# Two store streams move from ScalarE's to SyncE's DMA queue, and the planner of the order gets spare time

## The chip, the cores and the metric

The kernel runs on one core of a Trainium2 chip. The metric is device time in microseconds (us) of one execution; the median of three runs before is 1178.59 us (1177.14 to 1179.32). The profiled execution took 1177.89 us, and its span, from the first to the last instruction of the program, is 1176.0 us. The engines are named as the profile names them: PE (matmul), DVE (VectorE), ACT (ScalarE), POOL (GpSimd) and SP (SyncE, which computes nothing here and only issues DMAs).

## The reference

Two layers, each applied twice in the order A, B, A, B with residual sums, on `x` of 2048 tokens by 640 channels, in float32:

```python
def _A_ref(x, wqkv, wo):            # 32 heads of 20, W, dil = 8, 2
    q, k, v = split(x @ wqkv)
    idx = pos[:, None] - dil * arange(W)[None, :]          # 8 keys, two tokens apart
    logits = einsum("bhsd,bhswd->bhsw", q, k[idx]) * scale  # masked where idx < 0
    o = einsum("bhsw,bhswd->bhsd", softmax(logits), v[idx])
    return o @ wo

def _B_ref(x, w1, b1, w2, b2):      # 640 -> 1536 -> 640
    h = gelu(layernorm(x) @ w1 + b1)
    return h @ w2 + b2

x = A_x
x = x + _A_ref(layernorm(x), A_wqkv, A_wo)
x = x + _B_ref(layernorm(x), B_w1, B_b1, B_w2, B_b2)
...                                 # the same two lines once more
```

## The kernel before

**Tiling.** A layer's tokens are cut into four units: even and odd tokens (the dilation is two) by two halves of 512 tokens each. With two rounds of layers there are eight units, n = 0 to 7, and a unit has four tiles (t = 0 to 3) of 128 tokens. Every float32 operand of a matmul is split into a high and a low float16 part and the product is made of three passes, so that one logical product over 640 channels is 15 matmuls.

**One unit.** The normalized tokens are transposed by DMA into `yT` (from the tile `w`, L570). PE makes the projected values in four groups of heads (`qkvp`, L602, 15 matmuls each; n, t, g). ACT copies each product from PSUM (`ps`, three banks) to `ev` (three buffers, L617), and a store writes two token tiles of a group from `ev` to a DRAM buffer `spill` (`put`, L623; 8 per unit, 64 in all). A fetch reads them back with their halo into `qk` and `v` (L642), DVE computes the attention of a group G = 4n + g (L684 to L722), and the result is split into `ohl` (L732). Its four tiles are transposed by DMA into `yT` (`oT`, L745), PE multiplies by `wo` (`wop`, L756, eight products of 15 matmuls per unit, through the same three banks `ps`), and DVE adds each product to the residual `xf` (L762). A layer norm follows and again a transposition (L570), and then the unit's MLP: per block of 128 hidden channels a first product (`hp`, L810, its weights in `c1`), GELU and the split on ACT and DVE (L816, L819, L821), and a second product into accumulators (`out`, L831, weights in `c2`).

**Weights of the MLP.** In the first 170 us or so the 24 blocks of `w1` and `w2` are loaded (L451), split into two float16 parts by ACT and DVE (L425, L426) into `c1` and `c2`, and stored to the DRAM buffers `mw` (L467, in `prep_m`; 24 stores). From then on the MLP loads its blocks from there into three buffers each (L803, 216 loads).

**What sets the order.** The instructions of all units are not issued where the code makes them: `Plan.run` collects them as operations with an engine, a duration, a priority and what they need, and lays them out on a time axis. It takes the engine and operation that can start first. The operations are then issued in the order of these planned starts. Each engine works its own list strictly in order, and waits at an instruction until what this needs is there. For a DMA the planner assumes a time from its issue to its first packet (`REACH`), a rate that transfers in flight share (`SHARE` when two queues are at work), and a time from the last packet to the landing (`LAND`). An operation that needs a transfer is planned for the landing (`start`, with `LAG["sp"]` = 0.05 us). These figures are the planner's; on the chip only the order remains of them.

**Queues.** DMAs are issued from SP (loads, fetches, transpositions, outputs) and from ACT (the 64 `put` and the 24 `mw` stores), so that a store's wait for its data stands in ACT's list, and every other DMA's wait in SP's.

Of the kernel before, what the change touches and what calls it, by code (L numbers as in the profile page):

```python
# [64 lines left out]
class Plan:  # L65
# [9 lines left out]


    AHEAD = 3.0
    REACH = 0.45
    LAND = 1.4

    SHARE = 1.15

    LETS = ("pv", "hlo", "lo", "at", "xb")

# [24 lines left out]
    def run(self):  # L109
        when = {}  # L110
        waiting = {}
        ready = {}
        left = {}
        for o in self.ops:
            left[o["n"]] = len(set(o["need"]))
            for k in set(o["need"]):
                waiting.setdefault(k, []).append(o)
            if not left[o["n"]]:
                ready.setdefault(o["eng"], []).append(o)
        clock = {e: 0.0 for e in self.LAG}  # L120
        table = None
        port, shut, before = 0.0, [], None
        order = []


        soon, queues, late = [], {}, []
        seen = 0.0

        def done(o, end, lag):
            for u in o["use"]:  # L130
                self.users[u] -= 1
                self.last[u] = max(self.last.get(u, 0.0), end + lag * (u[0] != "pr" or o["eng"] != "dve"))
                if not self.users[u]:
                    self.free[u[0]].append((self.last[u], self.slot[u]))
            for k in o["give"]:
                when[k] = (o["eng"], end, bool(o["move"]))
                for w in waiting.pop(k, ()):
                    left[w["n"]] -= 1
                    if not left[w["n"]]:
                        ready.setdefault(w["eng"], []).append(w)  # L140

        def heads():
            return [q[0] for q in queues.values() if q]

        def turn():
            h = heads()
            return sum(x[1] for x in h) * (self.SHARE if len(h) > 1 else 1.0)

        def event():

            h = heads()
            return min([b for b, _ in soon] + [e for e, _ in late]
                       + ([seen + max(0.0, min(x[0] for x in h)) * turn()] if h else []), default=math.inf)

        def advance(t):
            h = heads()
            if h:
                turns = (t - seen) / turn()
                for x in h:
                    x[0] -= turns  # L160
            for x in h:
                if x[0] < 1e-9:
                    queues[x[2]["eng"]].pop(0)
                    late.append((t + self.LAND, x[2]))
            for b, o in [v for v in soon if v[0] <= t]:
                soon.remove((b, o))
                queues.setdefault(o["eng"], []).append([*o["move"], o])
            for e, o in [v for v in late if v[0] <= t]:
                late.remove((e, o))
                done(o, e, self.LAG["sp"])  # L170
            return t

        def start(o):
            t = clock[o["eng"]]
            if o["lazy"]:
                t = max(t, seen - self.AHEAD + sum(x[0] * x[1] for q in queues.values() for x in q)
                        + sum(v["move"][0] * v["move"][1] for _, v in soon))
            if o["pair"] and o["eng"] == "dve":
                t = max(t, port)
            for k in o["need"]:  # L180
                e, w, moved = when[k]
                w = w + (self.LAG["sp"] if moved else self.LAG[e] if e != o["eng"] else 0.06 * (e != "pe"))
                t = max(t, w)
            if o["pair"] and o["eng"] == "pool":
                for i, (a, b) in enumerate(reversed(shut)):
                    if t >= b:
                        break
                    if a <= t:
                        t = b + 0.1 * (i == 0)
                        break  # L190
            new = {}
            for u in o["use"]:
                if u in self.slot:
                    t = max(t, self.since[u])
                else:
                    fs = self.free[u[0]]
                    if u[0] in self.ORDERED and self.line[u[0]][self.turn.get(u[0], 0)] != u:
                        return None
                    i = new.get(u[0], 0)
                    if i >= len(fs):  # L200
                        return None
                    t = max(t, sorted(fs)[i][0])
                    new[u[0]] = i + 1
            return t

        total = len(self.ops)
        while len(order) < total:
            best = None
            for e, ops in ready.items():
                pick = None  # L210
                for o in ops:
                    t = start(o)
                    if t is None:
                        continue
                    key = (max(t - o["wait"], clock[e] + 0.05), o["prio"], o["n"])
                    if pick is None or key < pick[0]:
                        pick = (key, t, o)
                if pick and (best is None or (pick[1], pick[0]) < (best[1], best[0])):
                    best = pick
            then = event()  # L220
            if best is None and then == math.inf:
                raise RuntimeError(f"the plan is stuck: {[u for u in self.slot if self.users[u]]}")
            if best is None or then <= best[1]:
                seen = advance(then)
                continue
            _, t, o = best
            e = o["eng"]
            ready[e].remove(o)
            d = o["dur"]
            if o["table"] and o["table"] != table:  # L230
                table = o["table"]
                d += self.SWITCH
            for u in o["use"]:
                if u not in self.slot:
                    fs = self.free[u[0]]
                    fs.sort()
                    self.turn[u[0]] = self.turn.get(u[0], 0) + 1
                    self.since[u], self.slot[u] = fs.pop(0)
            o["at"] = t
            order.append(o)  # L240
            clock[e] = t + d
            if o["move"]:
                soon.append((t + self.REACH + 0.2 * (o["dur"] > 1), o))
                continue
            if e == "dve":
                kind = o["give"][0][0]
                if o["pair"]:
                    if shut and t - shut[-1][1] < 0.05 and before != "pv" and kind not in self.LETS:
                        shut[-1][1] = t + d
                    else:  # L250
                        shut.append([t, t + d])
                before = kind
            elif e == "pool" and o["pair"] and d > 1:
                port = t + d
            done(o, t + d, self.LAG[e])
        order.sort(key=lambda o: o["at"])
        self.time = max(clock.values())
        self.order = order
        return order
# [15 lines left out]
def sliding_dilated_then_mlp_kernel(  # L275
# [99 lines left out]
        plan.add(by, 0.1 if by == "act" else 0.38, prio, emit, need, give, use, move=(kb * 1e3 / 16 / packet, packet_time(packet)), lazy=lazy)  # L375

    def dma_transpose(prio, emit, need=(), give=(), use=()):
        plan.add("sp", 1.45, prio, emit, need, give, use, move=(80, packet_time(256) + 0.0045))

    def mm(cols, n, prio, emit, need=(), give=(), use=()):  # L380
        plan.add("pe", cols / 2400.0 + 0.0028 * n, prio, emit, need, give, use)
# [80 lines left out]
    def prep_m(f, i, prio):  # L462
        ck = (f"c{i + 1}", ("prep", f))
        src = (lambda: B_w2[f * P:(f + 1) * P]) if i else (
            lambda: B_w1.rearrange("(k p) c -> p k c", p=P)[:, :, f * P:(f + 1) * P])
        prep_rows(("m", f, i), prio, src, lambda: tile_of(*ck)[:, 0], lambda: tile_of(*ck)[:, 1], [ck])
        dma(328, prio - 5, lambda: nc.scalar.dma_start(mw[i][f], tile_of(*ck)),  # L467
            need=[("lo", ("m", f, i))], give=[("mw", f, i)], use=[ck], by="act")

    def turn(prio, t, name, key, nk, yk):  # L470

# [113 lines left out]
    def qkv(n):  # L585
# [6 lines left out]
        for k, (g, b) in enumerate(halves):  # L592
# [27 lines left out]

            def put(g=g, b=b, ek=ek):
                to = spill[la][par]
                nc.scalar.dma_start(  # L623
                    bass.AP(tensor=to.tensor, offset=to.offset + (g * 3 * ROWS + HALO + start + 2 * b) * GC,
                            ap=[[M * GC, P], [ROWS * GC, 3], [1, 2 * GC]]),
                    tile_of(*ek).rearrange("p a t c -> p a (t c)"))

            dma(P * 6 * GC * 4 / 1e3, -310 + n, put, need=[("ev", n, 2 * b + i, g) for i in range(2)],
                give=[("put", n, g, b)], use=[ek], by="act", packet=8 * GC)

    def fetch(G):
        n, g = divmod(G, NG)
# [319 lines left out]
```

## Time and profile before

| | before |
|---|---|
| median of three runs | 1178.59 us (1177.14 to 1179.32) |
| the profiled execution | 1177.89 us |
| its span | 1176.0 us |
| PE busy | 1157.5 us, 98% |
| DVE busy | 991.6 us, 84% |
| ACT busy | 511.5 us, 43% |
| POOL busy | 150.9 us, 13% |
| granted TensorE clock | 0.998 |

PE is busy in almost every slice of the span, and DVE nearly so until about 990 us, when the last attention is done. Since each engine's list is fixed, the profile is read for the places where PE stands still: what it waited for, and where that was in the lists of DVE and SP. The chain of waits and the list of PE's waits give the places, and the timelines of PE, DVE and SP around each place tell why.

### The profile page before, as it was taken

The page shows a single profiled execution, that of the slowest core. Times are in us where ns is not written, and L with a number is a line of the kernel's source. Part 1 is how long each engine was busy: PE and PEld are TensorE (multiplying, and loading weights), DVE is VectorE, ACT ScalarE, POOL GpSimd, SP SyncE. Part 2 cuts the span into 40 slices and gives each one's busy share as a digit, 9 for nine tenths or more (in the row PEclk, how much of TensorE's full clock was granted, in tenths as well). Part 3 has the DMA queues.
Part 4 walks back from the last instruction along what each step waited for, and adds up shares of the span by engine and source line. Part 5 has one row for each costly group of instructions (what it writes and reads, how often), then busy time and mean ns, then how long its engine had stood idle before and what let it go on. Part 6 is the DMA issues. An engine that isn't in the chain of part 4 may idle for free.

```text
span 1176.0 us, 17291 instructions
## 1 busy us (share of the span) xinstructions
PE 1157.5 (98%) x6902; PEld 626.5 (53%) x6902; DVE 991.6 (84%) x939; ACT 511.5 (43%) x925; POOL 150.9 (13%) x96
## 2 busy tenths in 40 slices
PE   8999999999999999999999999999999999999998
PEld 5444445577554455545554555555456555555554
DVE  7899999999899999999999999999999996311211
ACT  5485334436445345732537352376235423512121
POOL 1020102023011201320221012002120100000000
PEclk9999999999999999999999999999999999999999
DMA  9999997787776477567755865576555845633432
GB/s 294 300 329 283 373 349 195 212 269 243 210 205 196 162 215 188 176 191 190 193 180 177 212 167 188 202 166 186 188 177 161 246 158 128 154 103 102 145 101 79
DMA packets 219773, 235.01 MB, mean 200 GB/s; under 512 B 129884, under 2 KB 170412, under 8 KB 219692
## 3 DMA queue, kind: packets, MB, share of 16 engines
q1 hardware_dynamic: 190636, 194.57, 56.7%
q10 hardware_dynamic: 29056, 39.33, 9.6%
q8 instruction: 54, 0.88, 0.3%
q14 instruction: 27, 0.22, 0.1%
HBM read 158.93 MB, written 44.78 MB: 173 GB/s over the span
## 4 chain that ended last, share of the span: by engine, by line
PE 55%; DVE 28%; DMA 6%; issue 6%; ACT 4%; SPq 1%; POOL 0%; ACTq 0%; DVEq 0%; POOLq 0%
PE ps L602 20%; PE acc L831 14%; PE ps L810 14%; PE ps L756 7%; DVE pr L684 6%; DVE pr L710 6%; DVE pr L718 4%; DVE sm L688 4%; DMA yT<-w 2%; DVE act L821 1%; DMA qk<-spill 1%; ACT junk L528 1%; DMA act<-in_B_w_dram 1%; DVE w L722 1%; ACT junk L524 1%
## 5 line engine op out<-in xcount | busy, mean ns | idle before, releaser
L602 PE MATMUL ps<-wq,yT 128*128 128x480 f16 x1920 | 393.0, 367 | 4.8 <-DMA yT<-w 3.6
L831 PE MATMUL acc<-c,act 128*128 128x512 f16 (+1 forms) x2310 | 331.3, 299 | 1.1 <-DVE act L821 0.6
L810 PE MATMUL ps<-yT,c 128*128 128x512 f16 (+1 forms) x1620 | 328.6, 355 | 0.8 <-DMA c<-mw 0.8
L602 PEld LDWEIGHTS <-yT 128*128 128x128 f16 x1920 | 187.7, 98 | 207.0 <-DMA yT<-w 5.1
L831 PEld LDWEIGHTS <-act 128*128 128x128 f16 x2310 | 181.7, 98 | 143.3 <-DVE act L821 1.2
L810 PEld LDWEIGHTS <-c 128*128 128x128 f16 x1620 | 154.5, 98 | 147.1 <-DMA c<-mw 1.2
L816 ACT ACTIVATE act<-ps,b 128x512 f32<-128x512 f32 (+1 forms) x108 | 68.7, 637 | 272.4 <-PE ps L810 268.0
L684 DVE TENSOR_TENSOR pr<-qk 128x2560 f32<-128x2560 f32 x64 | 181.5, 2836 | 4.1 <-DMA qk<-spill 4.1
L710 DVE TENSOR_TENSOR pr<-sm,v 128x2560 f32<-128x2560 f32 x64 | 179.7, 2819 | 0.2
L688 DVE TENSOR_REDUCE sm<-pr 128x128 f32<-128x2560 f32 x64 | 179.5, 2805 | 0.1
L821 DVE TENSOR_TENSOR act<-act 128x512 f16<-128x512 f32 (+1 forms) x108 | 72.3, 671 | 124.1 <-ACT act L819 123.8
L718 DVE TENSOR_TENSOR pr<-pr 128x1280 f32<-128x1280 f32 (+1 forms) x128 | 144.8, 1151 | 0.2
L756 PE MATMUL ps<-wo,yT 128*128 128x320 f16 x960 | 132.4, 299 | 5.9 <-DMA yT<-ohl 3.3
L617 ACT ACTIVATE ev<-ps 128x480 f32<-128x480 f32 x128 | 71.6, 563 | 148.8 <-PE ps L602 137.3
L756 PEld LDWEIGHTS <-yT 128*128 128x128 f16 x960 | 93.7, 98 | 44.4 <-DMA yT<-ohl 4.3
L732 POOL TENSOR_TENSOR ohl<-w,ohl 128x640 f16<-128x640 f32 x24 | 67.1, 2796 | 379.2 <-ACT ohl L729 379.2
L541 POOL TENSOR_TENSOR ln<-ln,half 128x2 f32<-128x2 f32 (+1 forms) x30 | 36.2, 1207 | 451.0 <-ACT ln L538 451.0
L524 ACT ACTIVATE junk<-xf 128x640 f16<-128x640 f32 x56 | 41.1, 734 | 79.2 <-DVE xf L762 60.3
L819 ACT ACTIVATE act<-act 128x512 f16<-128x512 f32 (+1 forms) x108 | 62.4, 580 | 2.6
L568 DVE TENSOR_TENSOR w<-w,w 128x640 f16<-128x640 f32 x60 | 51.2, 874 | 1.5 <-ACT w L566 1.5
L560 ACT ACTIVATE w<-xf,ln 128x640 f32<-128x640 f32 x56 | 49.7, 908 | 1.9 <-DVE w L568 1.6
L566 ACT ACTIVATE w<-w 128x640 f16<-128x640 f32 x60 | 42.7, 727 | 12.5 <-DVE w L568 7.2
(53 smaller groups left out, 515.1 us busy)
## 6 DMA issues: line engine op xcount, KB each, us to landing
c<-mw SPq DMA_DIRECT2D x216, 320.0 KB, 3.2
spill<-ev ACTq DMA_DIRECT2D x64, 480.0 KB, 4.3
qk<-spill SPq DMA_DIRECT2D x32, 880.0 KB, 5.5
v<-spill SPq DMA_DIRECT2D x32, 880.0 KB, 4.5
qk<-spill SPq DMA_DIRECT2D x32, 320.0 KB, 3.2
act<-in_B_w_dram SPq DMA_DIRECT2D x24, 320.0 KB, 5.9
mw<-c ACTq DMA_DIRECT2D x24, 320.0 KB, 5.8
xf<-in_A_x_dram SPq DMA_DIRECT2D x16, 320.0 KB, 6.3
```

The lines of the kernel that those rows point to most:

```text
L602: nc.tensor.matmul(ps, transposed(yk)[:, a * KD + k, t * P:(t + 1) * P], wq[:, b, k, g], start=first and j == 0, stop=last and j == len(to ...
L617: act(3 * GC, -400 + n, lambda i=i, pk=pk, ek=ek: nc.scalar.activation(tile_of(*ek)[:, :, i], tile_of(*pk)[:, :3 * GC].rearrange("p (a c) ...
L684: nc.vector.tensor_mul(tile_of(*pk), w[:, HALO + m + t0:HALO + m + t0 + EH, None, :].to_broadcast([P, EH, W, GC]), windows(w, t0, [GC, W], ...
L688: dve(E, G - 0.7, lambda pk=pk, t0=t0: nc.vector.tensor_reduce(lg(t0, t0 + EH).rearrange("p t w h -> p (t w h)"), tile_of(*pk).rearrange(" ...
L710: nc.vector.tensor_mul(tile_of(*vk).rearrange("p t w (h d) -> p t (w h) d", d=DH), lg(t0, t0 + EH).rearrange("p t w h -> p t (w h)")[:, :, ...
L718: dve(EH * w * GC, G - 0.9, lambda vk=vk, w=w: nc.vector.tensor_add(tile_of(*vk)[:, :, 0:w], tile_of(*vk)[:, :, 0:w], tile_of(*vk)[:, :, w ...
L732: eng.tensor_sub(tile_of(*hk)[:, :, 1, g * GC:(g + 1) * GC], ot(), hi())
L756: nc.tensor.matmul(tile_of(*pk)[:, :D // 2], transposed(yk)[:, a * KD + k, t * P:(t + 1) * P], wo[:, b, k, c * D // 2:(c + 1) * D // 2], s ...
L810: nc.tensor.matmul(tile_of(*pk)[:, :nt], tile_of(*ck)[:, a, k * P:(k + 1) * P], transposed(yk)[:, c * KD + k, t0 * P:t1 * P], start=i == 0 ...
L816: act(nt, -430, lambda pk=pk, h32=h32, e=e: nc.scalar.activation(tile_of(*h32)[:, :nt], tile_of(*pk)[:, :nt], AF.Gelu_apprx_tanh, bias=b1[ ...
L821: dve(nt, -1000, lambda h32=h32, hk=hk: nc.vector.tensor_sub(tile_of(*hk)[:, 1, :nt], tile_of(*h32)[:, :nt], tile_of(*hk)[:, 0, :nt]), nee ...
L831: nc.tensor.matmul(accs[k][:, c0:c0 + n], tile_of(*hk)[:, a, (i - t0) * P:(i - t0 + 1) * P], tile_of(*wk)[:, c, w0:w0 + n], start=first, s ...
```

## The change

Four things are edited.

1. The planner's figures for DMAs: a transfer starts `REACH` = 0.75 us after its issue (or its issue's own duration, if longer) plus a ramp of 0.2 us, lands 0.9 us after its last packet (0.5 us for a transposition) plus 0.7 us before what it used is free, and two queues share at 1.08 in place of 1.15. A transposition's issue is planned at 1.75 us in place of 1.45.
2. Spare time: an operation that needs a transfer is planned 2.0 us after the landing on PE, and 0.7 us after it on ACT, DVE and POOL.
3. The 64 stores of projected values (`put`) are issued from SP.
4. The 24 stores of split weights (`mw`) are issued from SP.

What each instruction computes is unchanged; the lists' order and the queue of 88 stores change. The number of instructions is the same on each engine but for the 88 that go from ACT to SP.

```diff
     AHEAD = 3.0
-    REACH = 0.45
-    LAND = 1.4
-
-    SHARE = 1.15
+    REACH = 0.75
+    LAND = 0.9
+    RAMP = 0.2
+
+    SPARE = {"pe": 2.0, "act": 0.7, "dve": 0.7, "pool": 0.7, "sp": 0.0}
+
+    SHARE = 1.08
...
-                    late.append((t + self.LAND, x[2]))
+                    late.append((t + self.LAND - 0.4 * (x[2]["dur"] > 1), x[2]))
...
-                queues.setdefault(o["eng"], []).append([*o["move"], o])
+                queues.setdefault(o["eng"], []).append([o["move"][0] + self.RAMP / o["move"][1], o["move"][1], o])
...
-                done(o, e, self.LAG["sp"])
+                done(o, e, 0.7)
...
-                w = w + (self.LAG["sp"] if moved else self.LAG[e] if e != o["eng"] else 0.06 * (e != "pe"))
+                w = w + (self.LAG["sp"] + self.SPARE[o["eng"]] if moved else self.LAG[e] if e != o["eng"] else 0.06 * (e != "pe"))
...
-                soon.append((t + self.REACH + 0.2 * (o["dur"] > 1), o))
+                soon.append((t + max(self.REACH, o["dur"]), o))
...
     def dma_transpose(prio, emit, need=(), give=(), use=()):
-        plan.add("sp", 1.45, prio, emit, need, give, use, move=(80, packet_time(256) + 0.0045))
+        plan.add("sp", 1.75, prio, emit, need, give, use, move=(80, packet_time(256) + 0.0045))
...
-        dma(328, prio - 5, lambda: nc.scalar.dma_start(mw[i][f], tile_of(*ck)),
-            need=[("lo", ("m", f, i))], give=[("mw", f, i)], use=[ck], by="act")
+        dma(328, prio - 5, lambda: nc.sync.dma_start(mw[i][f], tile_of(*ck)),
+            need=[("lo", ("m", f, i))], give=[("mw", f, i)], use=[ck])
...
             def put(g=g, b=b, ek=ek):
                 to = spill[la][par]
-                nc.scalar.dma_start(
+                nc.sync.dma_start(
...
             dma(P * 6 * GC * 4 / 1e3, -310 + n, put, need=[("ev", n, 2 * b + i, g) for i in range(2)],
-                give=[("put", n, g, b)], use=[ek], by="act", packet=8 * GC)
+                give=[("put", n, g, b)], use=[ek], packet=8 * GC)
```

The lines of the changed kernel stand three further down than before (L745 becomes L748). What moved is shown at three places.

**SP, ahead of the projection of unit 5** (`oT` of unit 5 is the L745 row; `c` tiles are MLP weights, `qk` and `v` the fetches of groups 26 and 25, `yT2` the tokens of unit 7). Before:

```order
L803 DMA c12_80<-mw05_116 128x1280
L803 DMA c20_81<-mw13_126 128x1280
L803 DMA c10_78<-mw06_117 128x1280
L642 DMA qk0_67<-spill11_138 128x640
L642 DMA qk0_67<-spill11_138 128x1760
L803 DMA c21_82<-mw14_127 128x1280
L745 DMA_TRANSPOSE yT0_72<-ohl0_75 128x10x128 x4
L570 DMA_TRANSPOSE yT2_74<-w3_87 128x10x128
```

With the change:

```order
L806 DMA c12_80<-mw05_116 128x1280
L806 DMA c20_81<-mw13_126 128x1280
L748 DMA_TRANSPOSE yT0_72<-ohl0_75 128x10x128 x4
L645 DMA qk0_67<-spill11_138 128x640
L645 DMA qk0_67<-spill11_138 128x1760
L573 DMA_TRANSPOSE yT2_74<-w1_85 128x10x128
L806 DMA c21_82<-mw14_127 128x1280
L573 DMA_TRANSPOSE yT2_74<-w0_84 128x10x128
```

The four transpositions now stand ahead of two weight loads and of the two parts of a fetch, behind which they stood.

**DVE, ahead of unit 4's projected values** (the L568 rows are the last step before the transposition of its first two token tiles; L821 belongs to the MLP, L710 to L722 to the attention of group 7). Before:

```order
L710 TENSOR_TENSOR pr1_77<-sm1_90,v0_68 128x2560
L821 TENSOR_TENSOR act_66<-act_66 128x256
L718 TENSOR_TENSOR pr1_77<-pr1_77 128x2x640
L821 TENSOR_TENSOR act_66<-act_66 128x256
L718 TENSOR_TENSOR pr1_77<-pr1_77 128x2x320
L722 TENSOR_TENSOR w0_84<-pr1_77 128x320
L710 TENSOR_TENSOR pr0_76<-sm1_90,v0_68 128x2560
L821 TENSOR_TENSOR act_66<-act_66 128x256
L568 TENSOR_TENSOR w2_86<-w4_88,w2_86 128x640
L568 TENSOR_TENSOR w1_85<-w3_87,w1_85 128x640
```

With the change:

```order
L713 TENSOR_TENSOR pr0_76<-sm1_90,v0_68 128x2560
L571 TENSOR_TENSOR w2_86<-w0_84,w2_86 128x640
L824 TENSOR_TENSOR act_66<-act_66 128x256
L571 TENSOR_TENSOR w4_88<-w1_85,w4_88 128x640
L721 TENSOR_TENSOR pr0_76<-pr0_76 128x2x640
L824 TENSOR_TENSOR act_66<-act_66 128x256
L721 TENSOR_TENSOR pr0_76<-pr0_76 128x2x320
```

Both steps moved ahead of six instructions of the attention and the MLP. On PE, the products of unit 4 moved ahead of two pairs of MLP blocks (the second products of blocks 5 and 6 and the first products 20 and 21, 256 tokens wide) at the same place.

**SP, ahead of the MLP part of unit 1** (`yT0` rows are that unit's four transpositions for it; `c` are the weights of the running MLP part, `spill<-ev` the stores of projected values of unit 4). Before, the stores were in ACT's list:

```order
L642 DMA v0_68<-spill01_136 128x1760
L570 DMA_TRANSPOSE yT0_72<-w0_84 128x10x128
L570 DMA_TRANSPOSE yT0_72<-w1_85 128x10x128
L642 DMA qk0_67<-spill01_136 128x640
L642 DMA qk0_67<-spill01_136 128x1760
L570 DMA_TRANSPOSE yT0_72<-w4_88 128x10x128
L570 DMA_TRANSPOSE yT0_72<-w0_84 128x10x128
L803 DMA c21_82<-mw110_133 128x1280
L803 DMA c11_79<-mw01_112 128x1280
```

With the change:

```order
L645 DMA v0_68<-spill01_136 128x1760
L573 DMA_TRANSPOSE yT0_72<-w1_85 128x10x128
L573 DMA_TRANSPOSE yT0_72<-w3_87 128x10x128
L626 DMA spill10_137<-ev2_71 128x3x320
L806 DMA c22_83<-mw18_131 128x1280
L806 DMA c12_80<-mw011_122 128x1280
L806 DMA c20_81<-mw19_132 128x1280
L806 DMA c10_78<-mw00_111 128x1280
L573 DMA_TRANSPOSE yT0_72<-w1_85 128x10x128
L806 DMA c21_82<-mw110_133 128x1280
L573 DMA_TRANSPOSE yT0_72<-w3_87 128x10x128
L806 DMA c11_79<-mw01_112 128x1280
```

A store, four weight loads and no fetch now stand between the second and the third of these transpositions, and the weights of the running part are issued between transpositions that wait for DVE.

## Prediction, made before the changed kernel was run

> **What bounds the kernel now.** I read the busy shares first, then the list of PE's waits, then the timelines around each wait.
>
> ```profile
> span 1176.0 us, 17291 instructions
> PE 1157.5 (98%) x6902; PEld 626.5 (53%) x6902; DVE 991.6 (84%) x939; ACT 511.5 (43%) x925; POOL 150.9 (13%) x96
> 800.00:900.00 100.00, 99.16 (x560) 52.08 (x559) 98.75 (x84) 41.44 (x69) 19.10 (x9) 1.00 0.60 185
> ```
>
> The last row is one stretch of the span, with PE, PEld, DVE, ACT and POOL busy in that order. PE is the bound, and DVE runs beside it at nearly 99% as long as there is attention left. The matmuls are the same before and after the change, so the time moves by what PE stands still, 1176.0 - 1157.5 = 18.5 us, and by the clock it runs at. PE's waits by what ended them (us in total, times, longest):
>
> ```profile
> PE ps L602 <- DMA yT<-w: 3.6, 3, 2.0
> PE ps L756 <- DMA yT<-ohl: 3.3, 2, 2.5
> PE ps L756 <- DVE xf L762: 2.6, 3, 0.9
> PE ps L810 <- DMA c<-mw: 0.8, 1, 0.8
> ```
>
> 7.7 us are waits for a DMA to land, in six places; 2.6 us are waits for DVE to empty a bank `ps`, in three; the rest is the head, small gaps, and 3 us behind the last matmul. The six, on PE, each with its wait at the row's end:
>
> ```profile
> 233.62 1.81 PE L810 MATMUL ps<-yT,c 128*128 128x256 f16 x15 [0.85 <-DMA c<-mw]
> 296.68 7.94 PE L602 MATMUL ps<-wq,yT 128*128 128x480 f16 x30 [1.97 <-DMA yT<-w]
> 424.39 3.84 PE L756 MATMUL ps<-wo,yT 128*128 128x320 f16 x27 [0.83 <-DMA yT<-ohl]
> 502.59 2.60 PE L602 MATMUL ps<-wq,yT 128*128 128x480 f16 x12 [1.25 <-DMA yT<-w]
> 645.98 1.19 PE L602 MATMUL ps<-wq,yT 128*128 128x480 f16 x5 [0.35 <-DMA yT<-w]
> 787.44 12.81 PE L756 MATMUL ps<-wo,yT 128*128 128x320 f16 x93 [2.47 <-DMA yT<-ohl]
> ```
>
> The second of them costs more than its wait. The stretch behind it (PEclk is the number behind POOL's):
>
> ```profile
> 297.30:300.70 3.40, 3.40 (x10) 1.32 (x9) 3.40 (x3) 0.00 (x0) 0.00 (x0) 0.51 1.16 344
> ```
>
> For 3.4 us the granted clock was 0.51: half of 3.4 is 1.7 us lost. It is the only such stretch between the head and the tail.
>
> **The change, part by part.** *The projection of unit 5 (2.47 us).* DVE and SP ahead of it:
>
> ```profile
> 763.22 0.83 DVE L732 TENSOR_TENSOR ohl<-w,ohl 128x640 f16<-128x640 f32 x1 [0.27 <-ACT ohl L729]
> 759.01 16.55 SPq L803 DMA_DIRECT2D c<-mw  x6
> 778.03 0.80 SPq L642 DMA_DIRECT2D qk<-spill  x2
> 779.41 9.84 SPq L745 DMA_TRANSPOSE yT<-ohl  x4
> ```
>
> The data were ready at 764.1, and the first transposition was issued at 779.4, behind weight loads that wait for PE to free a buffer, one in some 3.25 us, and a fetch that waits for DVE. It landed 8.0 us later, at 787.4. In the new list the four stand behind the fifth of the six loads (759.01 + 4 x 3.25 = 772.0) and ahead of the sixth and the fetch. Issue at 772.3 and the median landing of its kind
>
> ```profile
> yT<-w SPq DMA_TRANSPOSE x60, 4.4
> yT<-ohl SPq DMA_TRANSPOSE x32, 3.8
> c<-mw SPq DMA_DIRECT2D x216, 320.0 KB, 3.2
> ```
>
> give 776 to 777. PE comes at 787.4 - 2.5 = 785.0, less one second product of the MLP that now stands behind (3.26 us, a row below): 781.7. The whole 2.47 goes.
>
> *Unit 4's projected values (1.97 us and the slow stretch).*
>
> ```profile
> 282.13 0.42 DVE L821 TENSOR_TENSOR act<-act 128x256 f16<-128x256 f32 x1
> 289.90 1.55 DVE L568 TENSOR_TENSOR w<-w,w 128x640 f16<-128x640 f32 x2
> 852.52 3.24 PE ps L810 x15
> 855.75 3.26 PE acc L831 x24
> ```
>
> DVE's first step moves to where the 282.13 row stands, 289.90 - 282.13 = 7.8 us earlier. PE arrives two pairs of half-width blocks earlier; a full-width pair is 3.24 + 3.26, so two halves are 6.5. The lead grows by 1.3: 0.7 of the wait stays. The slow stretch came behind a wait of 1.97, and none came behind 1.25 or less; behind 0.7 I expect none, and take the 1.7 as gone (bounds: nothing, and 1.7). The Trainium skill, "TensorE: Matmul & The Clock Gate", section "Part 1: The HAM clock gate (the "warmup" mystery)", has the clock halved only after at least one idle window of about 3.4 us. The 0.51 row stands behind an idle time of 1.97, so rule and row differ on the threshold, while the row's length of 3.4 us is the window's. By the rule alone no wait here would have cost clock, the term were nothing and the sum 1174.3.
>
> *The MLP's weights at 233 us (0.85).* The load was issued late, behind a fetch of `v` for which SP waited on DVE. In the new DVE list the step that frees `v` stands ahead of two instructions of 2.8 us, so SP is past it in time: I take 0.85 as gone. *Units 2 and 6 (0.83, 0.35).* The new lists give 0.7 and 1.2 us more lead: 0.6 and 0.35 go. *Unit 5's projected values (1.25).* DVE's step stands 4.2 us later in DVE's list and the products 2.2 later in PE's, 2.0 worse; against it DVE is 2 to 3 us earlier by then, since this idle time of DVE is filled with two instructions of the next group:
>
> ```profile
> 306.69 0.49 DVE L762 SCALAR_TENSOR_TENSOR xf<-ps,xf 128x320 f32<-128x320 f32 x1 [3.12 <-PE ps L756]
> ```
>
> I leave the 1.25 as it is. Gone: 2.47 + 1.3 + 1.7 + 0.85 + 0.6 + 0.35 = 7.3 us.
>
> *The start of unit 1's MLP part (new).*
>
> ```profile
> 333.55 1.55 DVE L568 TENSOR_TENSOR w<-w,w 128x640 f16<-128x640 f32 x2
> 334.62 6.22 SPq L570 DMA_TRANSPOSE yT<-w  x2
> 347.14 3.40 PE L810 MATMUL ps<-yT,c 128*128 128x512 f16 x15
> ```
>
> DVE is ready at 335.1 and PE comes at 347.1, a lead of 12.0. In the new list 9.5 us more of DVE's work stand ahead (three instructions of 2.8 and some short ones), of which the filled 3.1 are won back; PE comes 1.6 later by its list and about 2.2 earlier by the waits gone before: 12.0 - 9.5 + 3.1 + 1.6 - 2.2 = 5.0. One transposition ahead on SP (about 1.6 us, between a fourth of the 9.84 above and less) and 4.4 to land are 6.0: PE waits about 1.0 more, between nothing and 2 (at the 3.1 of issue that two took here). The running part's weights, now issued between these transpositions, wait with them and are in the same 1.0.
>
> *The head.* ACT now splits the third piece of the first weights after it copies the first tokens, not before:
>
> ```profile
> 8.15 0.72 PE L481 MATMUL acc<-ident,w 128*128 128x128 f32 x5
> 8.61 0.87 ACT L425 ACTIVATE wq<-pr 128x800 f16<-128x800 f32 x1 [0.28 <-DMA pr<-in_A_wqkv_dram]
> 9.39 0.74 ACT L487 ACTIVATE yT<-acc 128x512 f16<-128x512 f32 x2
> 10.02 3.34 PE L602 MATMUL ps<-wq,yT 128*128 128x480 f16 x15 [1.15 <-ACT yT L487]
> 11.22 0.88 DVE L514 BATCH_NORM_STATS2 bn<-xf 128x6 f32<-128x320 f32 x2
> ```
>
> The copy can begin at 8.9; the split then ends at 8.9 + 0.74 + 0.87 = 10.5, and the first products start near 10.6, not 10.0. What paces the next tokens is DVE, whose split of the same piece (1.0 us) then ends at 11.5, not 11.2. I take +0.3, between nothing and 0.6.
>
> *The queues.*
>
> ```profile
> L623 ACTq DMA_DIRECT2D spill<-ev x64: 366/367/1044, 20.1 to 853.2; - x64
> ```
>
> 64 issues of 0.37 us, and 24 of the weights at about as much, 33 us in all, leave an engine that is busy 43% of the time and that PE seldom waits for: worth nothing. On SP, which waits more than it issues, the issue time is hidden in its waits. What may cost is that a store waits there for its copy, and everything behind it too; the copy comes about a microsecond behind its product, and most stores stand behind instructions that wait longer. I count nothing; rival B holds the other end. The 2.6 us of bank waits I leave; rival A holds theirs.
>
> **Sum.** -7.3 + 1.0 + 0.3 = -6.0 against the profiled execution's own 1177.89: 1171.9. The median of the runs stands 0.7 above that execution, so 1172.6, said as 1172.5.
>
> Does DVE allow it? At the last projection:
>
> ```profile
> 987.68 0.82 DVE L732 TENSOR_TENSOR ohl<-w,ohl 128x640 f16<-128x640 f32 x1 [0.80 <-ACT ohl L729]
> 988.57 5.99 SPq L745 DMA_TRANSPOSE yT<-ohl  x4
> 992.29 16.46 PE L756 MATMUL ps<-wo,yT 128*128 128x320 f16 x120
> ```
>
> From DVE's end at 988.5 to PE's start are 3.8 us, just a landing: PE can't come earlier here unless its list holds more work ahead, or DVE ends earlier. The new list sets a first product and a quarter of a second one ahead, 3.24 + 0.8 = 4.1 us. The other 1.9 must come from DVE, out of the 3.1 that are filled.
>
> **The rivals.**
>
> *A: the banks take it back (no change).* With three banks and products of 16.46 / 8 = 2.06 us, a residual add of DVE that is late by more than two products holds PE. The new DVE list sets instructions of 2.8 us between the adds of units 1 and 3, where short ones or none stood, and by the lists' shifts an add is then 0.3 to 1.8 us too late at five of the eight projections, some 4.5 us in all: 1172.6 + 4.5 = 1177.1. For it: the planner now believes that PE starts these products 2 us after the landing, and plans DVE's adds accordingly late. Against it: each of these shrinks by what DVE is ahead.
>
> *B: everything waits in SP's list (slower).* Place: the eleven entries of PE that a transposition feeds (the projections of units 1 to 7, the first products of 4 to 7). Price: a store that waits 1.2 us for its copy, with the transposition behind it, costs 1.2 there; with nine hit, and one slow stretch of 1.7, 1172.6 + 10.8 + 1.7 = 1185. It decides from 6.0 / 11 = 0.55 us per entry on. For it: the 15 us for which the transposition at 779 us stood behind others show that SP's list holds up ready work. Against it: only the stores next to a transposition count. The Trainium skill, "DMA: Bandwidth & Descriptors", section "Anatomy of one DMA — SWDGE (gpsimd) path", says that the DMA engines don't wait on semaphores and that every such wait is made by the issuing sequencer. The 779.41 row agrees, and by that rule each store takes its wait along into SP's list.
>
> *C: more goes.* If DVE's earlier time carries through, the other DMA and bank waits go as well: 7.7 + 2.6 - 5.6 = 4.7, and the 1.0 at unit 1: 1172.6 - 5.7 = 1167.
>
> That the change does nothing the chip can see has no chance of its own: the lists differ at the places named.
>
> **Chances.** Forecast 0.49 (its own range 1169 to 1177), A 0.21, B 0.16, C 0.14. A measurement of this kernel tells about 0.2%, 2.4 us, from no change, so 1176.2 to 1181.0 counts as the same. Faster: C, 0.44 of the forecast and 0.04 of A, 0.62. Same: 0.15 of A, 0.04 of the forecast, 0.01 of B, 0.20. Slower: B's rest, 0.02 of A and 0.01 of the forecast, 0.18. The range goes from C's end to what leaves out the larger half of B: 1167 to 1182.
>
> **What would show it.** Right: in PE's waits `yT<-ohl` falls from 3.3 to under 1, `yT<-w` from 3.6 to 1 to 3, with no wait of 2 us at unit 5's projection and no stretch at half clock near 300 us; the new wait is at the start of unit 1's MLP part. A shows as `xf L762` at 6 or more; B as waits on `yT` of 10 or more, with transpositions queued on SP behind L626 rows. I am wrong altogether if PE's waits fall as said and the span doesn't.

## The result, and the profile after

The median of four runs each went from 1178.95 to 1166.35 us, a ratio of 0.9893 (95% interval 0.9867 to 0.992): 12.6 us less, where 6 were forecast. The profiled execution took 1165.98 us, 11.9 less than the one before, and 0.4 less than its median.

The busy times and PE's list of waits after the change (engine, line, what it waited for; us in total, times, longest):

```profile
span 1164.2 us, 17345 instructions
PE 1154.4 (99%) x6902; PEld 625.6 (54%) x6902; DVE 992.3 (85%) x939; ACT 510.2 (44%) x923; POOL 166.8 (14%) x96
PE ps L605 <- ACT wq L428: 2.5, 1, 2.5
PE acc L888 <- POOL ident L400: 1.4, 1, 1.4
PE acc L834 <- DVE act L824: 1.3, 2, 0.8
PE ps L605 <- DMA yT<-w: 0.5, 1, 0.5
PE acc L834 <- DVE xf L869: 0.5, 1, 0.5
PE ps L759 <- DVE xf L765: 0.3, 1, 0.3
```

All line numbers are three higher than before. PE's idle time fell from 18.5 to 9.8 us and its busy time by 3.1, of which 1.7 is the half-clock stretch near 300 us, which is gone; the rest comes from several small differences. `yT<-ohl` went from 3.3 to nothing, `yT<-w` from 3.6 to 0.5, `c<-mw` from 0.8 to nothing, and the banks (`xf`, L762 before, L765 now) from 2.6 to 0.3. The first two rows are the head. Its waits are 3.9 us before (1.4, 1.3 and 1.2 in three rows) and 3.9 now, but in the profiled execution a stretch at half clock has come there that the one before did not have (stretch, length, busy time of PE, PEld, DVE, ACT and POOL with their counts, then the granted clock):

```profile
10.93:14.34 3.41, 3.41 (x10) 1.23 (x9) 3.04 (x10) 0.00 (x0) 1.24 (x2) 0.50 1.15 365
```

The first 15 products start 0.15 us earlier than before (9.87 against 10.02) and take 4.88 us instead of 3.34. PE has made up for it by 15.2 us, since it no longer waits for DVE in between (1.3 us before).

The places that the prediction spoke of, in the timeline after the change (start, duration, engine; a bracket at the end of a row is the engine's wait before it):

```profile
231.21 0.72 PE L834 MATMUL acc<-c,act 128*128 128x512 f16 x4 [0.79 <-DVE act L824]
286.34 15.35 PE L605 MATMUL ps<-wq,yT 128*128 128x480 f16 x75
334.93 0.83 DVE L571 TENSOR_TENSOR w<-w,w 128x640 f16<-128x640 f32 x1
343.47 4.70 PE L813 MATMUL ps<-yT,c 128*128 128x512 f16 x21
496.56 3.62 PE L605 MATMUL ps<-wq,yT 128*128 128x480 f16 x17 [0.53 <-DMA yT<-w]
764.26 6.40 SPq L748 DMA_TRANSPOSE yT<-ohl  x4
773.39 16.46 PE L759 MATMUL ps<-wo,yT 128*128 128x320 f16 x120
975.02 0.83 DVE L735 TENSOR_TENSOR ohl<-w,ohl 128x640 f16<-128x640 f32 x1 [0.80 <-ACT ohl L732]
984.54 5.73 PE L759 MATMUL ps<-wo,yT 128*128 128x320 f16 x41
```

Four rows of PE carry no bracket: unit 4's projected values (286.34) and unit 5's projection (773.39), which had 1.97 and 2.47 before, the start of unit 1's MLP part (343.47), where a new wait was forecast, and the last projection (984.54). A bracket of 0.53 stands at unit 5's projected values (1.25 before), and one of 0.79 (0.28 before) at the start of unit 0's MLP, on an activation that DVE splits late.

The last two rows matter most. DVE's last split ended at 988.5 before and ends at 975.85 now, 12.7 us earlier. PE began that projection at 992.29 and begins it at 984.54, 7.75 earlier, with more of its list ahead of it. The lead of DVE over PE there, from the end of its last split to PE's start, grew from 3.8 to 8.7 us.

Where DVE won its time is seen from its busy time in stretches up to its last split, before and after (stretch, us, DVE busy):

```profile
0.00:100.00 100.00, 86.26 (x111) 1.00 1.00 297
300.00:400.00 100.00, 94.28 (x87) 1.00 0.65 196
700.00:800.00 100.00, 96.50 (x85) 1.00 0.68 191
0.00:988.60 988.60, 953.17 (x880) 1.00 0.72 216
```

After the change, with PE, PEld, DVE, ACT and POOL in that order:

```profile
0.00:100.00 100.00, 96.16 (x519) 49.62 (x520) 90.60 (x113) 64.17 (x125) 15.03 (x21) 0.98 0.98 296
300.00:400.00 100.00, 99.96 (x611) 56.02 (x610) 99.46 (x91) 46.37 (x88) 24.73 (x10) 1.00 0.67 195
700.00:800.00 100.00, 100.00 (x607) 53.91 (x606) 99.45 (x93) 54.44 (x99) 19.80 (x11) 1.00 0.61 182
0.00:975.90 975.90, 969.93 (x5759) 527.36 (x5760) 953.83 (x880) 463.36 (x843) 165.46 (x94) 1.00 0.73 218
```

DVE's work is the same (953.2 and 953.8 us); its idle time ahead of the last split fell from 35.4 to 22.1, by 13.3. Of this, 4.3 lie in the first 100 us, 5.2 between 300 and 400, and 3.0 between 700 and 800. By what ended it, DVE's waits for PE's products of the projections fell by 4.5 up to the last split (7.3 to 2.8 us), those for fetches by 2.4 (4.1 to 1.7), and those for ACT's part of the split of `wo`, in the first 40 us, by 3.5; the rest is spread thin:

```profile
DVE wo L426 <- ACT wo L425: 3.9, 2, 2.8
```

```profile
DVE wo L429 <- ACT wo L428: 0.4, 1, 0.4
```

So about a third of the idle time that went had been a wait for PE.

### The profile page after: what moved, and what is told of

The parts are those of the page before. It is cut to its first block, busy times and chain, and to the rows that moved or that the text cites. A ratio compares the mean times of both kernels' runs of the same rounds, so it can differ in the third digit from the quotient of the medians.

```text
span 1164.2 us, 17345 instructions
## 1 busy us (share of the span) xinstructions
PE 1154.4 (99%) x6902; PEld 625.6 (54%) x6902; DVE 992.3 (85%) x939; ACT 510.2 (44%) x923; POOL 166.8 (14%) x96
## 4 chain that ended last, share of the span: by engine, by line
PE 89%; DVE 7%; issue 2%; DMA 1%; ACT 0%; SPq 0%; DVEq 0%; ACTq 0%
PE ps L605 33%; PE acc L834 23%; PE ps L813 23%; PE ps L759 11%; DVE pr L687 2%; DVE pr L713 1%; DVE pr L721 1%; DVE sm L691 1%; DVE act L824 1%; DMA pr<-in_A_wqkv_dram 1%; DVE xf L869 0%; DMA yT<-w 0%; DVE w L571 0%; DVE w L725 0%; DVE sm L704 0%
## 5 line engine op out<-in xcount | busy, mean ns | idle before, releaser
L735 POOL TENSOR_TENSOR ohl<-w,ohl 128x640 f16<-128x640 f32 x24 | 81.4, 3391 | 410.2 <-ACT ohl L732 410.2
L544 POOL TENSOR_TENSOR ln<-ln,half 128x2 f32<-128x2 f32 (+1 forms) x30 | 39.2, 1306 | 400.1 <-ACT ln L541 400.1
```

What stands on the lines that cost most here:

```text
L735: eng.tensor_sub(tile_of(*hk)[:, :, 1, g * GC:(g + 1) * GC], ot(), hi())
```

## The experiments

Three questions: which part of the change makes the gain; whether DVE or PE holds the end; and what the half-clock stretch hangs on. Ratios are against the kernel before, with 95% intervals.

**The queue alone.** Order of before; only the issuing engine of the two stores is changed, while the planner still takes them for ScalarE's:

```
-        dma(328, prio - 5, lambda: nc.scalar.dma_start(mw[i][f], tile_of(*ck)),
+        dma(328, prio - 5, lambda: nc.sync.dma_start(mw[i][f], tile_of(*ck)),
...
-                nc.scalar.dma_start(
+                nc.sync.dma_start(
```

> The order of before, word for word on every engine, but the 88 stores are issued by SyncE instead of ScalarE, at the same place of the common order. Theory 'order' (the new order with spare time makes the gain): 1176 to 1181, PE's waits on yT stay at 6.9 us and DVE's idle time up to its last split at 35. Rival 'queue' (the stores' way through SyncE makes it, by stores that leave sooner and a ScalarE that issues nothing): 1166 to 1172, waits on yT under 3. Rival B of the prediction (stores hold up what stands behind them on SP): 1182 or more.

0.9999 (0.9988 to 1.001). The stores' way is worth nothing, to within 0.1%.

**The order alone.** The reverse: the order of the change, and the two stores issued by `nc.scalar`.

> The order of the change, word for word on every engine, but the 88 stores are issued by ScalarE as before. Theory 'order': 1164 to 1169, PE's waits on yT under 1.5 us. Rival 'queue': 1172 or more, since ScalarE's 33 us of issues come back and the stores wait behind its activations.

0.9894 (0.9876 to 0.9912): the whole gain. In the landing times of the two kernels (KB each, median us to landing) the queue does show, first the order alone, then the change:

```profile
spill<-ev ACTq DMA_DIRECT2D x64, 480.0 KB, 4.5
```

```profile
spill<-ev SPq DMA_DIRECT2D x64, 480.0 KB, 3.4
```

In the order of the change a store lands 1.1 us sooner through SP's queue (in the order of before 0.4 us: 4.3 and 3.9), and the time is the same. The gain is the order of the instructions; the two stores matter only in that the planner counts them in another engine's list.

**No spare time.** The change with

```
-    SPARE = {"pe": 2.0, "act": 0.7, "dve": 0.7, "pool": 0.7, "sp": 0.0}
+    SPARE = {"pe": 0.0, "act": 0.0, "dve": 0.0, "pool": 0.0, "sp": 0.0}
```

> The change with all spare time at 0; the stores' queue and the new numbers for transfers stay. Theory 'order' in its narrow form (the spare time makes the gain): most of it goes, 1173 to 1181, PE's waits on yT 4 us or more. Rival 'constants' (the plan's new landing times do it, or the queue): 1164 to 1169.

0.9966 (0.9953 to 0.9979): a third of the gain. PE's waits of this kernel:

```profile
PE ps L759 <- DMA yT<-ohl: 4.0, 3, 2.0
PE ps L605 <- DMA yT<-w: 3.9, 2, 3.2
```

**Spare time on one side.** PE's 2.0 alone, and the other engines' 0.7 alone:

> The change, but spare time on TensorE alone (2.0 us; 0 elsewhere). Theory 'spare time on PE cures PE's waits for transpositions': PE's waits on yT under 1.5 us, against 7.9 with no spare time at all and 0.5 with all of it. The time is 1165 to 1172, with some more of DVE's waits for qk<-spill. Rival 'it is the engines' smaller spare time': yT 4 us or more, 1172 to 1178.

> The change, but spare time on ScalarE, VectorE and GpSimd alone (0.7 us; 0 on TensorE). Theory 'spare time on PE': PE's waits on yT 4 us or more, 1171 to 1180. Rival: under 1.5 us, 1165 to 1170.

0.9941 (0.9919 to 0.9963) and 0.9949 (0.9931 to 0.9968). The first is a miss: with PE's spare time alone PE's waits on `yT` stay at 6.8 us, 4.35 of them in front of unit 2's projection. DVE's last split for it ends at 420.5, 12 us later than in the change:

```profile
PE ps L759 <- DMA yT<-ohl: 6.8, 3, 4.4
```

```profile
419.66 0.82 DVE L735 TENSOR_TENSOR ohl<-w,ohl 128x640 f16<-128x640 f32 x1
427.19 1.25 PE L759 MATMUL ps<-wo,yT 128*128 128x320 f16 x4 [4.35 <-DMA yT<-ohl]
```

PE itself came there only 4.7 us later than in the change, wait left out, so that the 2 us by which the planner sets PE later did not cover it.

With the other engines' spare time alone the waits on `yT` are 5.1 us (2.9 on `yT<-ohl`, 2.2 on `yT<-w`), as expected. So neither side alone cures them.

**The planner's other edits.** The stores planned and issued on ScalarE (`by="act"`), with the new spare time and the new numbers; and a profile of the same kernel, for its waits:

> The change with its spare time and its numbers for transfers, but the stores planned and issued on ScalarE as before; so the plan is made anew, and its order differs from both. Theory 'order': 1164 to 1170, as any plan with this spare time. Rival 'queue': 1172 to 1179.

> The kernel planned with the spare time and with the stores on ScalarE, whose time equals that of before, for a look at its waits. If DMA waits are what spare time cures: PE's waits on yT under 2 us, and its loss stands elsewhere (banks, DVE, the clock), some 10 us. If spare time does not cure them: yT 5 us or more.

0.9997 (0.9983 to 1.0011): the gain is gone altogether. That is a miss: 1179.1 us, where any plan with this spare time was expected at 1164 to 1170. It doesn't speak for the rival either, since the queue alone is worth nothing. The profile has no wait on `yT` at all, as expected; the loss is elsewhere:

```profile
PE acc L834 <- DVE act L824: 6.7, 4, 2.8
PE ps L813 <- DMA c<-mw: 1.7, 3, 1.0
PE acc L834 <- DMA c<-mw: 1.4, 1, 1.4
```

These 9.8 us, and two half-clock stretches of 3.4 us behind the waits at 228 and 348 us (2 x 1.7 us), make up for what the transpositions no longer cost. Next, the change with the transfers' numbers of before (the issue and landing times of the diff above are set back as well):

```
-    REACH = 0.75
-    LAND = 0.9
-    RAMP = 0.2
+    REACH = 0.45
+    LAND = 1.4
+    RAMP = 0.0
...
-    SHARE = 1.08
+    SHARE = 1.15
```

> The change with its spare time and its stores on SyncE, but with the numbers for transfers of before (0.45 us to reach the queue, 1.4 to land, 1.15 for shared queues, a transposition's issue 1.45). Theory: PE's waits on yT under 1.5 us, as with any plan that has PE's spare time; whether the time is that of the change hangs on the rest of the order, which no theory foretells: 1164 to 1178. Rival 'the new numbers do it': yT 4 us or more, 1172 or above.

0.996 (0.9943 to 0.9976), with 2.4 us of waits on `yT` (expected under 1.5) and one wait of 4.0 on DVE at unit 0's MLP. And more spare time (3.0 on PE, 1.2 on DVE):

> The change with more spare time (3.0 us on TensorE, 1.2 on VectorE). If what is left of PE's waits is for late data: 1163 to 1166, yT and c<-mw at 0. If spare time is enough already and a larger one only sets DVE's work later for the banks and the units' MLP parts: 1166 to 1175, waits on DVE above 2 us.

0.9908 (0.9893 to 0.9923), 0.4 us on `yT`, no better than the change, with 4.9 us of waits on DVE: the second expectation. Together:

| planned with | PE waits on `yT`, us | ratio |
|---|---|---|
| the order of before | 6.9 | 1 |
| no spare time | 7.9 | 0.9966 |
| PE's alone | 6.8 | 0.9941 |
| the others' alone | 5.1 | 0.9949 |
| both, transfers of before | 2.4 | 0.996 |
| both, stores in ScalarE's list | 0 | 0.9997 |
| both, larger | 0.4 | 0.9908 |
| both: the change | 0.5 | 0.9893 |

The waits are those of one profiled execution of each plan, which lies up to 3.4 us from the median of its runs (with the stores in ScalarE's list, 0.9 us); they say where a plan waits, not what it takes. In these plans it takes spare time on both sides to cure the waits for transpositions. That alone doesn't give the time, since each new plan also waits elsewhere: by its list of waits, 6.7 us on DVE at the MLP with the stores in ScalarE's list, 4.0 there and 2.5 at the banks with the transfers of before. The queue alone gives nothing, and each edit to the plan that was taken away lost about half of the gain or more. Why the plan without the stores in SP's list is worse at the MLP parts was not followed up.

**One wait alone, and two.** In the order of before, only the four transpositions of unit 5's projection are moved ahead of the loads and the fetch they stood behind (rows of SP, shortened):

```
+ L745 DMA_TRANSPOSE yT<-ohl x4
  L803 DMA c<-mw  (three of them)
  L642 DMA qk<-spill x2
  L803 DMA c<-mw
- L745 DMA_TRANSPOSE yT<-ohl x4
```

> The order of before but for four rows on SP: the transpositions of unit 5's projection stand ahead of the three weight loads and the fetch they were queued behind. Theory 'DVE follows' (DVE waits for PE where PE waits for DMA, so that a wait taken from PE moves DVE as well and the gain reaches the end): 2.5 less than before, the span as well; DVE's last split 2.3 earlier; no new wait behind. Rival 'DVE is fixed' (the prediction's step: DVE's last split stays where it is, and PE waits later for what it does not wait for here): 0 to 0.8 less than before, with some 2 us of new waits on yT<-ohl or on the banks behind 790 us.

0.9963 (0.9952 to 0.9974), 4.4 us less, where 2.5 were expected. The profile shows 2.65 of them. Up to the place PE runs 1.6 us later than before (longer waits for a bank at 195 us and for the MLP's weights at 234 us), and behind it 1.1 earlier, with no wait at unit 5's projection:

```profile
767.48 6.17 SPq L745 DMA_TRANSPOSE yT<-ohl  x4
786.37 8.86 PE L756 MATMUL ps<-wo,yT 128*128 128x320 f16 x64
```

DVE does the same: 1.6 us later up to the place, 1.1 earlier behind it. The step comes at its residual add, which before had waited for the product that waited for the transpositions, and now waits no more (before, then here):

```profile
789.69 0.49 DVE L762 SCALAR_TENSOR_TENSOR xf<-ps,xf 128x320 f32<-128x320 f32 x1 [2.27 <-PE ps L756]
```

```profile
788.88 0.49 DVE L762 SCALAR_TENSOR_TENSOR xf<-ps,xf 128x320 f32<-128x320 f32 x1
```

From there on PE and DVE both keep their 1.1 to the end: DVE's last split ended at 987.4 instead of 988.5. The interval, 3.1 to 5.7 us, does not reach down to 2.65; the rest was not followed up.

Next, unit 4's projected values alone: DVE's two splits ahead of one product of 2.8 us, their transpositions ahead of a fetch and two loads.

> The order of before but for unit 4's projected values: DVE's two splits for them stand ahead of one product of 2.8 us and one short step, and their transpositions ahead of the fetch of v and two weight loads on SP. Both theories: the wait of 1.97 us goes. Theory 'the half-clock stretch hangs on this wait': it goes too, 3.7 less than before in all, no stretch at half clock near 300 us. Rival 'the stretch comes anyway' (set by how PE was busy before, not by the wait): 2.0 less. Rival 'DVE is fixed': 0 to 1 less, new waits on yT behind 300 us.

0.9984 (0.9971 to 0.9997), 1.9 us less: the size that the rival 'the stretch comes anyway' gave, though not at its place. The wait of 1.97 and the stretch at half clock near 300 us are gone; 1.11 comes back at the next projection. What is left of it moves DVE as well: across the place PE gains 2.7 us on the order of before and DVE 2.6. And a stretch at half clock has come at another place, behind the wait of unit 5's projection, where before had none:

```profile
781.38:784.79 3.41, 1.32 (x10) 0.99 (x11) 1.78 (x3) 0.74 (x1) 0.00 (x0) 1.00 1.38 164
784.79:788.20 3.41, 3.41 (x15) 1.90 (x14) 1.76 (x2) 0.00 (x0) 0.00 (x0) 0.50 1.11 210
```

Both corrections together:

> Both corrections of the two kernels before, in the order of before. If waits taken from PE add up and reach the end: 6.1 us less than before. If DVE holds the end: 0 to 2 less. What this leaves of the change's 12 us is owed to the rest of the order (the banks, the smaller waits, DVE's idle time).

0.9959 (0.9944 to 0.9973), 4.8 us less: between the two expectations and nearer to the sum (6.1), which lies within its interval, with a new wait of 1.4 at unit 1's projection. In its profile PE gains 2.2 us across the one place and 2.6 across the other. At the last projection:

```profile
985.45 0.83 DVE L732 TENSOR_TENSOR ohl<-w,ohl 128x640 f16<-128x640 f32 x1 [0.80 <-ACT ohl L729]
986.33 6.00 SPq L745 DMA_TRANSPOSE yT<-ohl  x4
990.05 2.20 PE L756 MATMUL ps<-wo,yT 128*128 128x320 f16 x15
```

DVE's end and PE's start are both 2.2 us earlier than before, and the lead is still 3.8. DVE moves with PE. By the ratios the two waits are worth somewhat less than half of the change; no run isolates the rest. It is not that DVE's earlier time clears the banks: the waits for a bank are 3.1 us here, and were 2.6 before:

```profile
PE ps L756 <- DVE xf L762: 3.1, 3, 1.4
```

**Has DVE slack at the end?** Two row sums of unit 7's attention are done twice, 5.6 us more of DVE's work, once in the order of before and once in that of the change:

```
     for o in plan.run():
         o["emit"]()
+        if o["give"][0] in (("lg", 30, 1), ("lg", 31, 0)):
+            o["emit"]()
```

> The kernel before, with two of unit 7's row sums on VectorE run twice: 5.6 us more of VectorE's work ahead of the last projection, nothing else changed. If VectorE has no slack at the last projection (lead 3.8 us, of which all is the landing): 4.5 to 5.6 us slower, as a wait of PE on yT<-ohl there. If the lead says nothing (VectorE's idle time or PE's list takes it): under 1.5 us slower.

> The changed kernel with the same two row sums run twice, 5.6 us more of VectorE's work. If the new order left VectorE slack (lead 8.7 less a landing of 3.8 is 4.9): 0 to 1.5 us slower than the changed kernel, so 1166 to 1168. If VectorE holds the end there too: 4.5 to 5.6 slower, 1171 to 1172.

In the order of before 1.0063 (1.0039 to 1.0087), 7.4 us slower (4.6 to 10.3 by the interval), where 4.5 to 5.6 were expected. The last projection waits:

```profile
991.86 0.83 DVE L732 TENSOR_TENSOR ohl<-w,ohl 128x640 f16<-128x640 f32 x1 [0.80 <-ACT ohl L729]
992.75 6.08 SPq L745 DMA_TRANSPOSE yT<-ohl  x4
996.26 7.01 PE L756 MATMUL ps<-wo,yT 128*128 128x320 f16 x38 [4.64 <-DMA yT<-ohl]
```

4.64 us of wait, and half clock for 3.4 us behind it (1.7). The profiled execution took 1183.55 us and one more 1183.1, at a granted clock of 0.997; three others took 1187.3 to 1187.7, at 0.993. The difference in the clock, 0.004 of 1187, is about the 4 us between them, so that the size above the expected one goes with the clock.

In the order of the change 0.9913 (0.9894 to 0.9933) against the change's own 0.9893 (0.9867 to 0.992): 2.2 us more by the medians, a little above the expected 1.5; 1.2 by the profiled executions; and not told apart by the intervals. The last projection doesn't wait:

```profile
980.60 0.82 DVE L735 TENSOR_TENSOR ohl<-w,ohl 128x640 f16<-128x640 f32 x1 [0.80 <-ACT ohl L732]
985.74 16.46 PE L759 MATMUL ps<-wo,yT 128*128 128x320 f16 x120
```

DVE ends there 5.6 us later than in the change, and PE begins 1.2 later with no bracket. Of the 1.2, 0.4 was there ahead of the added work; the other 0.8 arises at 919.6 us, where PE waits for a residual add of the MLP that stands behind the first of the doubled sums. So in the order of before DVE had no slack at its last split. In the new one it has about 5 us there (the lead of 8.7 less the 3.8 of a landing), though not at every product that it feeds.

## Why the prediction was right and wrong

**The waits on DMAs: right, in part by luck.** Of the 7.3 us forecast as gone, 7.7 went: 2.47 at unit 5's projection (2.47), 1.97 at unit 4's values (1.3), 1.7 of half clock (1.7), 0.83 at unit 2's projection (0.6), 0.35 at unit 6's values (0.35), and at unit 0's MLP 0.85 of weights, against which a wait on DVE grew from 0.28 to 0.79 (0.85 forecast, 0.34 left). Moving the transpositions was the right reading of unit 5, as its one correction alone shows. The 1.7 of half clock came out by luck: the reason given for it, a length of wait between 1.25 and 1.97 from which the clock falls, doesn't hold (last section), and in the run with unit 4 corrected such a stretch came back at another place.

**The step that failed: DVE's time, in "Does DVE allow it?" and in the terms that use it.** The prediction let DVE win back 3.1 us, the one idle time it had read (at 306 us), and held its last split fixed but for these. That DVE has no slack there in the order of before was right: 5.6 us of added work cost 4.64 of wait. What was wrong is the size of what DVE wins. By the start of unit 1's MLP part its idle time had fallen by 7.6 us (22.6 to 15.0), and by its last split by 13.3 (35.4 to 22.1). Its end was taken as DVE's own, while a part of its idle time was a wait for PE: taking one wait from PE moved DVE's end by the same amount (2.65 in the run with unit 5 corrected, from 1.55 later to 1.10 earlier). That part is 4.5 of the 13.3; the others, as the 3.5 for the split of `wo`, are owed to the new lists, and no run isolates them.

**Where the forecast falls short.** In the profile it does by 5.8 us (6.0 against 11.8 of the span). *The start of unit 1's MLP (1.0):* the new wait didn't come; DVE's split there ended at 334.93 + 0.83 = 335.8, 5.7 earlier than reckoned, and PE came at 343.5, 3.0 earlier, a lead of 7.7 where 5.0 were reckoned and 6.0 needed. This term hangs on the step. *Unit 5's projected values (0.7):* "I leave the 1.25" became 0.53, for which DVE's earlier time is the likely reason, not a shown one. *The banks (2.3):* the 2.6 us "I leave" fell to 0.3. This is a failure of its own: the prediction gave no reason why they should stay, and DVE's earlier time is not the cause that the runs show, since with both corrections DVE ends 2.2 us earlier and the banks still cost 3.1. What differs is where the adds stand in DVE's list. A residual add that begins 4.4 to 4.6 us behind the end of its product stood before each of the three waits; with both corrections, and so the lists of before, they are 4.4 to 5.0; in the new order no add begins later than 3.8. *The head (0.4 to 0.5):* +0.3 was forecast, and by 15.2 us PE was 0.2 earlier; this has nothing to do with the step. 0.4 more are in the DMA waits. The last 0.9 are not in the lists of waits; PE's busy time fell by 1.4 beside the half-clock stretch, and more of it could not be placed.

**The rivals.** C came nearest: "if DVE's earlier time carries through, the other DMA and bank waits go as well", with 1167 as its price. DVE's earlier time did carry through, and these waits went, but for the banks the reason is another, so that its price fits in part by luck. Its chance of 0.14 was too low, and the range ended at its price, 0.65 us above what came. A (the banks take it back) and B (everything waits in SP's list) are refuted: the banks fell to 0.3, and with the stores in SP's list at the old places the time is the same to 0.1%.

**The queues: right.** ScalarE's 33 us of issues were counted at nothing, and the run with the queue alone gives nothing.

**What would show it.** `yT<-ohl` fell below 1 and the half-clock stretch near 300 us went, as said; `yT<-w` fell further than said; the new wait at unit 1's MLP was the sign that failed.

## What to carry to other kernels

Where two engines wait for each other in turn, neither one's end is a bound for the other: sum up the idle time of both up to the point where they meet, and test the slack by adding work to one of them. A wait that stands in the profile can be worth its length at the end where the engine that feeds it had been waiting as well; in the run with unit 4 corrected 1.11 of 1.97 came back at the next projection. Numbers of a planner that sets an order are not additive: taking any one edit away made another order, so judge the order that comes out and not the edits.

## What the hardware showed

**The half-clock stretches start on a fixed grid.** In each profile all changes of the granted clock lie whole multiples of 3.413 us apart (from 297.3 us to the tail at 1174.6 there are 257 of them; from 235.0 to 1173.7 in the run with unit 5 corrected, 275), and a stretch follows one such window in which PE did little. So what counts is how much of a wait falls into one window. The window ahead of a stretch, in the run with unit 5 corrected, and then one ahead of none, though the wait (1.94 us) was longer than the first's (1.46):

```profile
231.63:235.04 3.41, 1.61 (x12) 0.62 (x10) 3.41 (x8) 0.89 (x2) 0.00 (x0) 1.00 0.98 395
235.04:238.45 3.41, 3.41 (x16) 2.29 (x17) 2.86 (x2) 0.78 (x2) 2.37 (x1) 0.50 0.50 182
296.48:299.89 3.41, 1.81 (x17) 1.39 (x15) 2.88 (x6) 1.51 (x3) 0.00 (x0) 1.00 1.13 317
299.89:303.30 3.41, 3.07 (x16) 1.50 (x17) 3.41 (x3) 0.00 (x0) 0.00 (x0) 1.00 1.08 343
```

With the queue alone, a wait of 2.8 us fell on two windows and cost no clock:

```profile
782.57:785.98 3.41, 1.69 (x14) 0.77 (x10) 3.41 (x4) 2.35 (x4) 0.00 (x0) 1.00 1.33 204
785.98:789.39 3.41, 2.34 (x18) 1.70 (x19) 0.81 (x2) 0.74 (x1) 0.00 (x0) 1.00 0.99 213
```

Over the profiles of both kernels and of all runs whose clock was full outside such stretches, from 4 to 1160 us, each of the ten windows with 1.32 us or less of PE's busy time in it was followed by half clock and none with 1.69 or more; between 1.39 and 1.61 both occurred. A window already at half clock with 2.33 us busy was followed by another one, in the run with PE's spare time alone. The grid stands differently against the start from profile to profile (windows begin at 7.52 us after the change, at 8.03 with the same order and the stores on ScalarE), so whether a wait of some 1.5 to 3 us costs 1.7 us more looks like chance. The prediction's reading, that a wait of 1.97 has a stretch behind it and one of 1.25 none, was too simple: before, the 2.47 at unit 5 had none, and a stretch came behind 1.46 in another run. The Trainium skill, "TensorE: Matmul & The Clock Gate", section "Part 1: The HAM clock gate (the "warmup" mystery)", says that the window is 3413 ns and free-running, with which the traces agree; its table puts the half clock behind at least one idle window, and here a window that was busy for up to 1.61 of its 3.41 us was idle enough.
